# A PSUM bank of its own for the accumulator that is read between block products, in a fused attention and feed-forward kernel

## The chip, the cores and the metric

One core of a Trainium2 chip runs the kernel. The metric is the device time in microseconds of one execution, as the median of several runs. Engines: PE is TensorE (matrix products), DVE is VectorE, ACT is ScalarE, POOL is GpSimd, SP issues the DMAs. PSUM is the memory into which PE writes its products; it has eight banks of 512 fp32 words in each of 128 partitions. SBUF is the working memory.

## The reference

```python
# q, k, v: 4 x 8 x 768 x 64; n_global 8, n_local 96
scores = q @ k.T / sqrt(64)
keep = is_global | is_local                # first 8 positions, or the last 96
scores = where(keep, scores - slope[h] * dist, -1e9)
a = softmax(scores)                        # with 1e-9 added to the sum
x = (a @ v) as 3072 x 512                  # tokens x heads
h = x @ w_in                               # 512 x 2048
g = h * 1 / (1 + exp(-1.702 * h))
out = g @ w_out                            # 2048 x 512, fp32
```

## The kernel before

The 3072 tokens are 24 blocks of 128 rows, two blocks a chunk, so twelve chunks. Every fp32 operand is split into two fp16 halves, high and low, and a product is three fp16 products (high x high, high x low, low x high).

Attention runs block by block: scores on PE (`s`, L522), bias and row minimum on DVE (L528, two passes for two heads), exponentials on ACT (L538), the split into halves on ACT and DVE (`hl`, L542, L543), a transposing DMA (`pt`), and the products with the values on PE (`pv`, L553 to L555). It runs some 60 us ahead of the feed-forward part of the same rows.

The feed-forward part takes each chunk through eight steps of 256 hidden columns. `up` makes `h`, ACT and DVE make the activation and its two halves `g`, and `down` adds its product with `w_out` to the two output accumulators `y` of the chunk (L898). The first three chunks take `up` as it stands. From chunk 3 on (`TWO`), `up_two` takes two steps at once as a 2 x 2 block product by a scheme with seven products in place of eight, the Winograd form: p1 to p7, each of twelve matmuls of 128 x 128. Sums of the blocks of `x` and of the weights are made beforehand (`sums`, `twist`: `xS` and `T`).

In `up_two` an accumulator is read while it is built: p1 is written to `a`, ACT copies it out (k1, L849), p6 is added onto it, ACT copies (k2, L840), p7 is added, DVE adds it to `h1` (q22, L843), p4 is added, and the activation reads it. In the same way p5 is written to `b`, copied (k5, L840), p3 is added, and DVE adds it to `h0` (q12, L843). p2 is only added to `h0` (q11, L843). `a` and `b` are the two halves of one PSUM buffer `ab`, one bank; p2 has a bank for itself. The two banks of a step pair come from the ring `h` or are the accumulators `y10` and `y11`, in turn. Instructions of different engines that touch one PSUM buffer are kept apart by semaphores, in the order in which the program lists them, whichever part of the buffer they touch.

The order is not written by hand. The kernel lists tasks, each with the engines that can do it and a time on each, the tasks it comes after, the buffers it uses and a wished-for time (`add`). `Work.order` goes through a made-up clock: at each moment it gives each free engine the task with the earliest due time among those whose predecessors have ended (plus `LAT`, 0.3, from one engine to another) and whose buffers are to be had. A ring holds so many buffers; a new one is to be had when the last user of the old one has ended. Nothing in that clock knows that two engines cannot be at one bank together. The tasks are then emitted in that order, so every engine's queue has it.

The last chunk's last `down` writes each `y` in two halves of 256 columns, so that the first half can go out earlier: `yo` on DVE or ACT (L912, L913) and a DMA from SP (L914). Both halves lie in one bank. At the end a check of the inputs' size is summed over partitions by one matmul (`pb`, L1052) and read as a flag; the general path behind the flag is not taken here.

Of the kernel before, what the change touches and what calls it, by code (L numbers as in the profile page):

```python
# [19 lines left out]
P = 128  # L20
# [22 lines left out]
class Ring:  # L43


    def __init__(self, pool, tag, bufs, loose=False):
        self.pool, self.tag, self.bufs, self.loose, self.line = pool, tag, bufs, loose, []


class Buf:  # L50


    def __init__(self, ring, shape, dtype, name):
        self.ring, self.shape, self.dtype, self.name = ring, shape, dtype, name
        self.users, self.left, self.end, self.t = [], 0, 0.0, None
        ring.line.append(self)

    def __call__(self):
# [17 lines left out]
class Work:  # L76
# [15 lines left out]
    def order(self):  # L92
# [25 lines left out]
        while len(done) < len(self.tasks) + spared:  # L118
            moved = False
            for e in free:  # L120
                if free[e] > now or (e == "SP" and dma > now + BACKLOG):
                    continue
                best = None
                for t, at in ready.items():
                    if e not in t.on or at > now or t.early() > now or (best is not None and t.due >= best.due):
                        continue
                    us = t.on[e]
                    if any(max(free[o], now) + c < now + us for o, c in t.on.items() if o != e):
                        continue
                    fits = True  # L130
                    for b in t.bufs:
                        if b.left == len(b.users):
                            r = b.ring
                            more = sum(x.left == len(x.users) for x in t.bufs[:t.bufs.index(b)] if x.ring is r)
                            old = r.taken[more - r.bufs] if len(r.taken) + more >= r.bufs > more else None
                            if (r.next != b.i and not r.loose) or (old is not None and (old.left or old.end > now)):
                                fits = False
                                break
                    if fits:
                        best = t  # L140
                if best is None:
                    if e != "PE" or now > WARM or now < worked + (GAP if worked > 7.0 else 0.0):
                        continue
                    best = self.spare(spared)
                    b = best.bufs[0]
                    if len(b.ring.taken) >= b.ring.bufs and (b.ring.taken[-b.ring.bufs].left or b.ring.taken[-b.ring.bufs].end > now):
                        continue
                    b.users, b.left = [best], 1
                    ready[best] = now
                    spared += 1  # L150
                t, us = best, best.on[e]
                del ready[t]
                for b in t.bufs:
                    if b.left == len(b.users):
                        b.ring.next += 1
                        b.ring.taken.append(b)
                t.eng, t.start = e, now
                if e == "SP":
                    free[e] = now + 0.1
                    dma = max(dma, now + 1.2) + us  # L160
                    t.end = dma + 1.0
                else:
                    free[e] = t.end = now + us
                    if e == "PE":
                        worked = t.end
                for b in t.bufs:
                    b.left -= 1
                    b.end = max(b.end, t.end)
                for n in t.next:
                    missing[n] -= 1  # L170
                    if not missing[n]:
                        ready[n] = max(a.end + (LAT if n.on.keys() != {a.eng} else 0.0) for a in n.after)
                done.append(t)
                moved = True
            if not moved:
                later = [x + 1e-6 for x in (t.early() for t in ready) if x > now]
                later += [x for x in (*free.values(), dma - BACKLOG + 1e-6) if x > now] + [at for at in ready.values() if at > now]
                later += [t.end for t in done[-64:] if t.end > now] + ([worked + GAP + 1e-6] if now < worked + GAP else [])
                assert later, "the tasks wait for each other"
                now = min(later)  # L180
        return done
# [13 lines left out]
def kernel(  # L195
# [54 lines left out]


    def ring(tag, bufs, pool=sb, loose=False):
        return Ring(pool, tag, bufs, loose)

    r_raw, r_qk16, r_QK, r_KG = ring("raw", 2), ring("qk16", 1), ring("QK", 3), ring("KG", 1)
    r_VR, r_VG, r_sm = ring("VR", 4), ring("VG", 1), ring("sm", 3)
# [554 lines left out]
    def up_two(c, S, want):  # L811
# [1 line left out]

        nm = f"{c}_{S}"
        rx, rz = (r_h, r_h) if S % 2 == 0 else (r_y[1, 0], r_y[1, 1])
        ab, p2 = Buf(rx, [P, 2, 2, P], F32, "ab" + nm), Buf(rz, [P, 2, P], F32, "p2" + nm)
        h0, h1 = Buf(r_VF, [P, 2, 2, P], F32, "h0" + nm), Buf(r_VF, [P, 2, P], F32, "h1" + nm)
        ts = [Buf(r_t, [P, 2, 2, P], F32, f"t{nm}_{t}") for t in range(2)]
        gg = [Buf(r_g, [P, 2, 2, 2, P], F16, f"g{nm}_{t}") for t in range(2)]
# [2 lines left out]
        half = lambda w, k: (w, lambda z: w()[:, z, 512 * k:512 * k + 512])  # L822
        (B11, B21), B22 = (half(W, 0), half(W, 1)), half(V, 1)
        (T1, T4), (T3, T2) = TT[S, 0], TT[S, 1]
        a, b = (lambda: ab()[:, 0]), (lambda: ab()[:, 1])
        wr = [W_ready[2 * S, 0], W_ready[2 * S + 1, 0], x_ready[2 * c], x_ready[2 * c + 1]]
        tr = [*T_ready[S], xS_ready[c]]

# [8 lines left out]
            return add({"PE": 12 * MM128}, mms, after, [ob, x, wk_[0]], want + due)  # L837

        def keep(o, src, sb_, sp_, after):
            return add({"ACT": 0.3}, lambda e: nc.scalar.copy(o(), src()), after, [sb_, sp_])  # L840

        def plus(o, src, sb_, sp_, after):
            return add({"DVE": 0.34}, lambda e: nc.vector.tensor_add(o(), src(), o()), after, [sb_, sp_])  # L843

        c11, c12 = (lambda: h0()[:, 0]), (lambda: h0()[:, 1])
        p1 = product(a, B11, X, 0, 0, wr, ab, 0.0, first=True)
        p5 = product(b, T1, Xs, 1, 1, [*tr, p1], ab, 0.7)
        p2_ = product(p2, B21, X, 1, 0, wr, p2, 1.4, first=True, last=True)
        k1 = add({"ACT": 0.3}, lambda e: nc.scalar.copy(c11(), a()), [p1, line.get("k1")], [h0, h1, ab])  # L849
        line["k1"] = k1  # L850
        k5 = keep(h1, b, h1, ab, [p5])
        p6 = product(a, T2, Xs, 0, 0, [*tr, k1], ab, 2.1)
        p3 = product(b, B22, Xs, 1, 0, [*tr, *wr, k5], ab, 2.8, last=True)
        q11 = plus(c11, p2, h0, p2, [k1, p2_])
        k2 = keep(c12, a, h0, ab, [p6])
        q12 = plus(c12, b, h0, ab, [k2, p3])
        p7 = product(a, T3, Xs, 0, 1, [*tr, k2], ab, 4.1)
        q22 = plus(h1, a, h1, ab, [p7, k5])
        p4 = product(a, T4, X, 1, 1, [*tr, *wr, q22], ab, 5.5, last=True)
        ups[c, 2 * S] = ups[c, 2 * S + 1] = [p1, p5, p2_, p6, p3, p7, p4]  # L860

        def swish(o, src, srcs, after, w):
# [3 lines left out]
                       [t1], srcs)  # L866

        u0 = [swish(ts[0], h0, [ts[0], h0], [q11, q12], 2)]
        u1 = [swish(lambda: ts[1]()[:, 1], h1, [ts[1], h1], [q22], 1), swish(lambda: ts[1]()[:, 0], a, [ts[1], ab], [p4], 1)]
        for t, u in enumerate((u0, u1)):  # L870
            g, tt = gg[t], ts[t]
            t4 = add({"ACT": 0.53}, lambda e, g=g, tt=tt: nc.scalar.mul(g()[:, 0], tt(), SG / (SX * SW)), u, [tt, g])  # L872
# [3 lines left out]

    def down_two(c, S, want):
        if S == 0:
            ys[c] = [Buf(r_y[0, t], [P, DM], F32, f"y{c}_{t}") for t in range(2)]
        for t in range(2):  # L880
            g, ready = gs[c, S, t]

# [4 lines left out]

    def pile(c, t, g, ready, part, steps, want):

        y, end, begin = ys[c][t], steps[-1] == NST - 1, steps[0] == 0  # L890
        parts = 2 if end and c == NCHUNK - 1 else 1
        w = DM // parts

        def mms(e, m):
            for f in range(2 * len(steps)):
                s = steps[f // 2]
                for j, (zg, z) in enumerate(((0, 0), (0, 1), (1, 0))):
                    nc.tensor.matmul(y()[:, m], part(zg, f), w2(s, z, f % 2)[:, m],  # L898
                                     start=(begin and f + j == 0 and m.start == 0),
                                     stop=(end and j == 2 and f == 2 * len(steps) - 1 and m.stop == DM), skip_group_check=True)  # L900

        f_ = 0.5 / (SG * SW)
        yo = Buf(r_t, [P, DM], F32, f"yo{c}_{t}") if end else None
        last = down_last.get((c, t))
        for p_ in range(parts):
            m = slice(p_ * w, p_ * w + w)
            t1 = add({"PE": 6 * len(steps) * MM512 / parts}, lambda e, m=m: mms(e, m), [*ready, last],
                     [g, y, *(WT[s, 1] for s in steps)], want)
            down_last[c, t] = t1
            if end:  # L910
                t2 = add({"DVE": 0.62, "ACT": 0.5} if parts == 1 else {"DVE": 0.35, "ACT": 0.3}, lambda e, m=m: (
                    nc.vector.tensor_scalar(yo()[:, m], y()[:, m], f_, None, ALU.mult) if e == "DVE" else  # L912
                    nc.scalar.mul(yo()[:, m], y()[:, m], f_)), [t1], [y, yo], want + 4)  # L913
                add({"SP": 0.7 / parts}, lambda e, m=m: nc.sync.dma_start(  # L914
                    out[(2 * c + t) * P:(2 * c + t + 1) * P, m], yo()[:, m]), [t2], [yo], want + 6)

    def down(c, s, want):
        if s == 0:
            ys[c] = [Buf(r_y[c % 2, t], [P, DM], F32, f"y{c}_{t}") for t in range(2)]
        g, ready = gs[c, s]  # L920
        for t in range(2):
            def part(zg, f, t=t):
# [94 lines left out]
    bad = fin[:, 0:1]  # L1017
    ones = const.tile([P, 1], F32, name="ones")
    nc.gpsimd.memset(ones, 1.0)
    pb = Buf(r_s, [P, 512], F32, "pb")  # L1020

    def rows_hold(e):
        nc.vector.tensor_scalar(NM[:, 0:EARLY], top, 1.0 / SC, None, ALU.mult)
# [245 lines left out]
```

## Time and profile before

| | us |
|---|---|
| median of 3 runs | 631.23 (631.23 to 631.97) |
| profiled execution, its own time | 631.02 |
| its span in the profile | 629.2 |
| PE busy | 601.2 (96%) |
| DVE busy | 505.3 (80%) |
| ACT busy | 480.4 (76%) |
| PE at `y`, L898 (1176 matmuls) | 268.2 |

The span runs from the first to the last instruction that the profile shows. Busy time of PE is the union of its matmuls, whose recorded ends are modelled: a matmul of 128 columns is recorded with 0.22 us, though the next starts 0.06 us later. Rows of the timeline give the start, the duration, the engine and line, output and inputs by tile name, the number of merged instructions, and in brackets the idle time ahead and what ended it. The rows of waits give who waited for whom: total, times and the longest, in us.

### The profile page before, as it was taken

How to read it: one execution, taken by the hardware profiler on the slowest of the kernel's cores; microseconds unless marked ns; L12 is line 12 of the kernel's file. 1: busy time of each engine (PE TensorE's matmuls, PEld its weight loads, DVE VectorE, ACT ScalarE, POOL GpSimd, SP SyncE). 2: the span in 40 equal slices, each digit the busy share in tenths (PEclk: the TensorE clock that was granted, in tenths of full speed). 3: DMA queues.
4: the chain of work that ended last, by engine and by line, in shares of the span. 5: the costliest groups of instructions: out<-in, count | busy, mean ns of one | idle time of the engine just before them, and what ended most of it. 6: DMA issues, size and time to landing. Idle time of an engine off the chain costs nothing. (4 is left out here: it accounts for less than half of the span.)

```text
span 629.2 us, 16979 instructions
## 1 busy us (share of the span) xinstructions
PE 601.2 (96%) x6799; PEld 446.9 (71%) x6802; DVE 505.3 (80%) x1176; ACT 480.4 (76%) x1099; POOL 3.9 (1%) x16
## 2 busy tenths in 40 slices
PE   7989998999999999999999999999999999999995
PEld 4877776776776768767668777677777677776663
DVE  5778899999999969778889979869888878766341
ACT  3678999878877978868988879978998977734331
POOL 2000000000000000000000000000000000000000
PEclk9999999999999999999999999999999999999999
DMA  8999797999687778699989999999999997610001
GB/s 192 278 239 321 224 282 148 200 193 167 147 156 131 143 125 158 120 200 194 184 175 221 205 213 192 201 209 188 199 252 204 200 225 168 118 19 2 34 3 37
DMA packets 260854, 108.00 MB, mean 172 GB/s; under 512 B 241665, under 2 KB 242177, under 8 KB 260769
## 3 DMA queue, kind: packets, MB, share of 16 engines
q1 hardware_dynamic: 260480, 106.85, 81.7%
q8 instruction: 54, 0.88, 0.6%
q14 instruction: 32, 0.25, 0.1%
q10 hardware_dynamic: 288, 0.00, 0.0%
HBM read 56.43 MB, written 6.29 MB: 100 GB/s over the span
## 5 line engine op out<-in xcount | busy, mean ns | idle before, releaser
L898 PE MATMUL y<-w,g 128*128 128x512 f16 (+1 forms) x1176 | 268.2, 375 | 0.9 <-DVE g L873 0.9
L898 PEld LDWEIGHTS <-g 128*128 128x128 f16 x1176 | 110.6, 98 | 107.7 <-DVE g L873 1.2
L835 PEld LDWEIGHTS <-w 128*128 128x128 f16 x1728 | 101.6, 98 | 9.3 <-issue 4.8
L835 PEld LDWEIGHTS <-T 128*128 128x128 f16 x1296 | 78.2, 98 | 12.6 <-issue 4.3
L538 ACT ACTIVATE p<-p,NM 128x256 f32<-128x256 f32 (+1 forms) x160 | 77.4, 486 | 5.7 <-DVE NM L528 5.7
L795 PE MATMUL h<-xT,w 128*128 128x256 f16 x576 | 69.7, 273 | 2.3 <-DVE xT L701 1.4
L835 PE MATMUL ab<-xS,T 128*128 128x128 f16 x972 | 67.3, 219 | 3.2 <-ACT h L840 2.2
L543 DVE TENSOR_TENSOR hl<-p,hl 128x512 f16<-128x512 f32 (+1 forms) x80 | 51.9, 648 | 17.2 <-ACT hl L542 16.8
L795 PEld LDWEIGHTS <-w 128*128 128x128 f16 x576 | 55.4, 98 | 12.0 <-issue 2.7
L528 DVE CUSTOM_DVE_ANT_0 p<-s,mm 128x256 f32<-128x256 f32 (+1 forms) x160 | 58.5, 400 | 6.8 <-PE s L522 6.6
L873 DVE SCALAR_TENSOR_TENSOR g<-t,g 128x512 f16<-128x512 f32 x72 | 49.4, 688 | 8.4 <-ACT g L872 7.7
L835 PE MATMUL ab<-xS,w 128*128 128x128 f16 x756 | 51.2, 219 | 3.6 <-ACT h L840 2.9
L872 ACT ACTIVATE g<-t 128x512 f16<-128x512 f32 x72 | 45.3, 630 | 9.5 <-DVE t L865 9.2
L864 ACT ACTIVATE t<-h 128x512 f32<-128x512 f32 (+1 forms) x72 | 36.3, 519 | 18.7 <-DVE h L843 18.6
L542 ACT CAST hl<-p 128x512 f16<-128x512 f32 (+1 forms) x80 | 47.0, 587 | 4.4 <-DMA pt<-hl 2.2
L865 DVE SCALAR_TENSOR_TENSOR t<-t,h 128x512 f32<-128x512 f32 (+1 forms) x72 | 39.1, 555 | 10.0 <-ACT t L864 9.6
L843 DVE TENSOR_TENSOR h<-ab,h 128x256 f32<-128x256 f32 x72 | 29.3, 420 | 14.7 <-PE ab L835 7.9
L522 PEld LDWEIGHTS <-QK 128*128 128x128 f16 x592 | 36.6, 98 | 5.3 <-DVE NM L528 2.7
L840 ACT COPY h<-ab 128x256 f32<-128x256 f32 x72 | 26.2, 371 | 16.2 <-PE ab L835 16.0
L522 PE MATMUL s<-QK 128*128 128x128 f16 x320 | 38.5, 219 | 0.0
L835 PE MATMUL ab<-xT,w 128*128 128x128 f16 x540 | 37.3, 219 | 0.0
L553 PE MATMUL pv<-VR,pt 128*128 128x64 f16 x288 | 33.8, 193 | 2.7 <-DMA pt<-hl 1.8
(190 smaller groups left out, 1074.4 us busy)
## 6 DMA issues: line engine op xcount, KB each, us to landing
ws<-in_moe_w_in_dram SPq DMA_DIRECT2D x8, 1024.0 KB, 6.1
ws<-in_moe_w_out_dram SPq DMA_DIRECT2D x8, 1024.0 KB, 8.1
raw<-in_q_dram SPq DMA_DIRECT2D x24, 256.0 KB, 4.1
raw<-in_k_dram SPq DMA_DIRECT2D x24, 256.0 KB, 4.8
QK<-QK SPq DMA_DIRECT2D x44, 128.0 KB, 4.3
out_dram<-yo SPq DMA_DIRECT2D x22, 256.0 KB, 3.0
raw<-in_v_dram SPq DMA_DIRECT2D x20, 256.0 KB, 3.7
ws_00again<-in_moe_w_in_dram SPq DMA_DIRECT2D x8, 512.0 KB, 5.1
```

The costliest lines, as they stand in the source:

```text
L522: nc.tensor.matmul(sp()[:, j, s * P:(s + 1) * P], d["QK"]()[:, 0, h, :], K[:, 1 + z, h, :], start=(z == 0), stop=(z == 1), skip_group_chec ...
L528: nc.vector.tensor_tensor_reduce(out=pr()[:, j, :], in0=sp()[:, j, :], in1=m, scale=-1.0 / SC, scalar=3.0e38, op0=ALU.add, op1=ALU.min, ac ...
L538: ex.append(add({"ACT": 0.28 + 0.105 * ns}, lambda e, j=j: nc.scalar.activation(pr()[:, j, :], pr()[:, j, :], AF.Exp, bias=NM[:, n, hs[j]: ...
L542: t4 = add({"ACT": 0.1 + 0.215 * ns}, lambda e: nc.scalar.copy(hl()[:, 0], pr()), ex, [pr, hl])
L543: t5 = add({"DVE": 0.07 + 0.265 * ns}, lambda e: nc.vector.tensor_sub(hl()[:, 1], pr(), hl()[:, 0]), [t4], [pr, hl])
L795: nc.tensor.matmul(ph()[:, fi, :], w1(s, cc, z, fi), X[:, y, cc, :], start=(j + cc == 0), stop=(j == 2 and cc == NCC - 1))
L835: nc.tensor.matmul(o()[:, fi], w, x()[:, y * NCC + 2 * k + cc, t], start=(first and fi + j + cc == 0), stop=(last and j + cc == 3), skip_g ...
L864: t1 = add({"ACT": 0.06 + 0.22 * w}, lambda e: nc.scalar.activation(o(), src(), AF.Tanh, scale=0.851 / (SX * SW)), after, srcs)
L865: return add({"DVE": 0.08 + 0.265 * w}, lambda e: nc.vector.scalar_tensor_tensor(o(), o(), 1.0, src(), ALU.add, ALU.mult), [t1], srcs)
L872: t4 = add({"ACT": 0.53}, lambda e, g=g, tt=tt: nc.scalar.mul(g()[:, 0], tt(), SG / (SX * SW)), u, [tt, g])
L873: t5 = add({"DVE": 0.61}, lambda e, g=g, tt=tt: nc.vector.scalar_tensor_tensor(g()[:, 1], tt(), SG / (SX * SW), g()[:, 0], ALU.mult, ALU.s ...
L898: nc.tensor.matmul(y()[:, m], part(zg, f), w2(s, z, f % 2)[:, m], start=(begin and f + j == 0 and m.start == 0), stop=(end and j == 2 and ...
```

## The change

`up_two` gets the buffers `pa` and `pb`, still two banks. `a` is `pa` alone; `pb` holds `b` and, as its second half `g_`, p2. p1 of a step pair also takes hold of `pb` and comes after p1 of the pair before. p6 and p3 are wished for earlier, p2 later, behind p5. The clock of `Work.order` learns of banks: for every PSUM buffer it notes until when PE, and until when the other engines, were at it (plus `LAT`), and a task of PE waits for the others and the reverse. Reads by ACT and DVE are not held apart in it. Some task times are set anew (0.26 for the copies).

In the last chunk each `y` has two buffers of 256 columns from the first step on, the second one in the banks of the rings `s` and `pv`, which are free by then. The check's sum takes its bank from the ring `h`.

```diff
+        self.bank = {}                                   # Buf
...
-                    fits = True
-                    for b in t.bufs:
+
+                    fits = all(b.bank.get(e != "PE", 0.0) <= now for b in t.bufs)
+                    for b in t.bufs if fits else ():
...
+                    if b.ring.psum:
+                        b.bank[e == "PE"] = max(b.bank.get(e == "PE", 0.0), t.end + LAT)
...
-        ab, p2 = Buf(rx, [P, 2, 2, P], F32, "ab" + nm), Buf(rz, [P, 2, P], F32, "p2" + nm)
+        pa, pb = Buf(rx, [P, 2, P], F32, "pa" + nm), Buf(rz, [P, 2, 2, P], F32, "pb" + nm)
...
-        a, b = (lambda: ab()[:, 0]), (lambda: ab()[:, 1])
+        a, b, g_ = pa, (lambda: pb()[:, 0]), (lambda: pb()[:, 1])
...
-            return add({"ACT": 0.3}, lambda e: nc.scalar.copy(o(), src()), after, [sb_, sp_])
+            return add({"ACT": 0.26}, lambda e: nc.scalar.copy(o(), src()), after, [sb_, sp_])
...
-        p1 = product(a, B11, X, 0, 0, wr, ab, 0.0, first=True)
-        p5 = product(b, T1, Xs, 1, 1, [*tr, p1], ab, 0.7)
-        p2_ = product(p2, B21, X, 1, 0, wr, p2, 1.4, first=True, last=True)
-        k1 = add({"ACT": 0.3}, lambda e: nc.scalar.copy(c11(), a()), [p1, line.get("k1")], [h0, h1, ab])
+        p1 = product(a, B11, X, 0, 0, [*wr, line.get("p1")], pa, 0.0, first=True)
+        p1.bufs.append(pb)
+        pb.users.append(p1)
+        line["p1"] = p1
+        p5 = product(b, T1, Xs, 1, 1, tr, pb, 0.7, first=True)
+        k1 = add({"ACT": 0.26}, lambda e: nc.scalar.copy(c11(), a()), [p1, line.get("k1")], [h0, h1, pa])
...
-        p6 = product(a, T2, Xs, 0, 0, [*tr, k1], ab, 2.1)
-        p3 = product(b, B22, Xs, 1, 0, [*tr, *wr, k5], ab, 2.8, last=True)
-        q11 = plus(c11, p2, h0, p2, [k1, p2_])
+        p6 = product(a, T2, Xs, 0, 0, [*tr, k1], pa, 1.4)
+        p3 = product(b, B22, Xs, 1, 0, [*tr, *wr, k5], pb, 2.1, last=True)
+        p2_ = product(g_, B21, X, 1, 0, [*wr, p5], pb, 2.8, last=True)
+        q11 = plus(c11, g_, h0, pb, [k1, p2_])
...
-            ys[c] = [Buf(r_y[0, t], [P, DM], F32, f"y{c}_{t}") for t in range(2)]
+            rings = [[r_y[0, t]] if c < NCHUNK - 1 else [r_y[0, t], (r_s, r_pv)[t]] for t in range(2)]
+            ys[c] = [[Buf(r, [P, DM // len(rs)], F32, f"y{c}_{t}{i}") for i, r in enumerate(rs)] for t, rs in enumerate(rings)]
...
-    pb = Buf(r_s, [P, 512], F32, "pb")
+    pb = Buf(r_h, [P, 512], F32, "pb")
```

Up to the first block product of chunk 3, some 205 us into the span, every engine has the same rows in both orders. PE in the last chunk, second step pair, before (the first matmul of each product alone; the buffer's name has the chunk and the pair): p1, p5, p2, p6, p3, `down`, p7.

```order
L835 MATMUL ab11_1_9680<-xT11_9048,w2_0_532 128x128
...
L835 MATMUL ab11_1_9680<-xS11_9436,T1_2130 128x128
...
L835 MATMUL p211_1_9710<-xT11_9048,w2_0_532 128x128
...
L835 MATMUL ab11_1_9680<-xS11_9436,T1_2130 128x128
...
L835 MATMUL ab11_1_9680<-xS11_9436,w3_0_711 128x128
...
L898 MATMUL y11_0_9754<-w0_1_353,g11_0_0_9644 128x512
```

The same stretch of PE's queue now: p1, p5, p2, p6, one half of the `down`, p3, p7.

```order
L839 MATMUL pa11_1_9680<-xT11_9046,w2_0_532 128x128
...
L839 MATMUL pb11_1_9695<-xS11_9504,T1_2130 128x128
...
L839 MATMUL pb11_1_9695<-xT11_9046,w2_0_532 128x128
...
L839 MATMUL pa11_1_9680<-xS11_9504,T1_2130 128x128
...
L905 MATMUL y11_00_9741<-w0_1_353,g11_0_0_9663 128x256
...
L839 MATMUL pb11_1_9695<-xS11_9504,w3_0_711 128x128
```

p3 followed p6 directly; now twelve half-wide matmuls of `down` stand between, and p6 and p3 are in different buffers.

DVE's end of queue before: the last activations and halves `g` of the last chunk, with one output piece `yo` in front of the last `g`.

```order
L843 TENSOR_TENSOR h111_3_10013<-ab11_3_9957,h111_3_10013 128x256
L865 SCALAR_TENSOR_TENSOR t11_3_1_10074<-t11_3_1_10074,h111_3_10013 128x256
L865 SCALAR_TENSOR_TENSOR t11_3_1_10074<-t11_3_1_10074,ab11_3_9957 128x256
L912 TENSOR_SCALAR yo11_0_10117<-y11_0_9754 128x256
L873 SCALAR_TENSOR_TENSOR g11_3_1_10115<-t11_3_1_10074,g11_3_1_10115 128x512
```

DVE's end of queue now:

```order
L847 TENSOR_TENSOR h111_3_10065<-pa11_3_10003,h111_3_10065 128x256
L872 SCALAR_TENSOR_TENSOR t11_3_0_10117<-t11_3_0_10117,h011_3_10038 128x512
L872 SCALAR_TENSOR_TENSOR t11_3_1_10120<-t11_3_1_10120,h111_3_10065 128x256
L880 SCALAR_TENSOR_TENSOR g11_3_0_10148<-t11_3_0_10117,g11_3_0_10148 128x512
L872 SCALAR_TENSOR_TENSOR t11_3_1_10120<-t11_3_1_10120,pa11_3_10003 128x256
L880 SCALAR_TENSOR_TENSOR g11_3_1_10165<-t11_3_1_10120,g11_3_1_10165 128x512
```

The output piece has left DVE's queue; all four stand on ACT, behind its last work on `g`.

More of the change, by code (lines that the diff above doesn't have):

```diff
@@ L43, with __init__ @@
 class Ring:
-    def __init__(self, pool, tag, bufs, loose=False):
-        self.pool, self.tag, self.bufs, self.loose, self.line = pool, tag, bufs, loose, []
+    def __init__(self, pool, tag, bufs, loose=False, psum=False):
+        self.pool, self.tag, self.bufs, self.loose, self.line, self.psum = pool, tag, bufs, loose, [], psum
 class Buf:
@@ L177, in order @@
                 later += [x for x in (*free.values(), dma - BACKLOG + 1e-6) if x > now] + [at for at in ready.values() if at > now]
-                later += [t.end for t in done[-64:] if t.end > now] + ([worked + GAP + 1e-6] if now < worked + GAP else [])
+                later += [x for t in done[-64:] for x in (t.end, t.end + LAT) if x > now] + ([worked + GAP + 1e-6] if now < worked + GAP else [])
                 assert later, "the tasks wait for each other"
@@ L252, in ring @@
     def ring(tag, bufs, pool=sb, loose=False):
-        return Ring(pool, tag, bufs, loose)
+        return Ring(pool, tag, bufs, loose, pool is ps)
     r_raw, r_qk16, r_QK, r_KG = ring("raw", 2), ring("qk16", 1), ring("QK", 3), ring("KG", 1)
@@ L845, in up_two @@
         c11, c12 = (lambda: h0()[:, 0]), (lambda: h0()[:, 1])
-        p1 = product(a, B11, X, 0, 0, wr, ab, 0.0, first=True)
-        p5 = product(b, T1, Xs, 1, 1, [*tr, p1], ab, 0.7)
-        p2_ = product(p2, B21, X, 1, 0, wr, p2, 1.4, first=True, last=True)
-        k1 = add({"ACT": 0.3}, lambda e: nc.scalar.copy(c11(), a()), [p1, line.get("k1")], [h0, h1, ab])
-        line["k1"] = k1
-        k5 = keep(h1, b, h1, ab, [p5])
-        p6 = product(a, T2, Xs, 0, 0, [*tr, k1], ab, 2.1)
-        p3 = product(b, B22, Xs, 1, 0, [*tr, *wr, k5], ab, 2.8, last=True)
-        q11 = plus(c11, p2, h0, p2, [k1, p2_])
[L855 to L859, printed above, removed]
+        p1 = product(a, B11, X, 0, 0, [*wr, line.get("p1")], pa, 0.0, first=True)
[4 more added lines that the diff above has]
+        k1 = add({"ACT": 0.26}, lambda e: nc.scalar.copy(c11(), a()), [p1, line.get("k1")], [h0, h1, pa])
+        line["k1"] = k1
+        k5 = keep(h1, b, h1, pb, [p5])
+        p6 = product(a, T2, Xs, 0, 0, [*tr, k1], pa, 1.4)
+        p3 = product(b, B22, Xs, 1, 0, [*tr, *wr, k5], pb, 2.1, last=True)
+        p2_ = product(g_, B21, X, 1, 0, [*wr, p5], pb, 2.8, last=True)
+        q11 = plus(c11, g_, h0, pb, [k1, p2_])
+        k2 = keep(c12, a, h0, pa, [p6])
+        q12 = plus(c12, b, h0, pb, [k2, p3])
+        p7 = product(a, T3, Xs, 0, 1, [*tr, k2], pa, 4.1)
+        q22 = plus(h1, a, h1, pa, [p7, k5])
+        p4 = product(a, T4, X, 1, 1, [*tr, *wr, q22], pa, 5.5, last=True)
         ups[c, 2 * S] = ups[c, 2 * S + 1] = [p1, p5, p2_, p6, p3, p7, p4]
@@ L868, in up_two @@
         u0 = [swish(ts[0], h0, [ts[0], h0], [q11, q12], 2)]
-        u1 = [swish(lambda: ts[1]()[:, 1], h1, [ts[1], h1], [q22], 1), swish(lambda: ts[1]()[:, 0], a, [ts[1], ab], [p4], 1)]
+        u1 = [swish(lambda: ts[1]()[:, 1], h1, [ts[1], h1], [q22], 1), swish(lambda: ts[1]()[:, 0], a, [ts[1], pa], [p4], 1)]
         for t, u in enumerate((u0, u1)):
@@ L888, in pile, with mms @@
     def pile(c, t, g, ready, part, steps, want):
[L890 to L894, printed above, removed]
+        end, begin = steps[-1] == NST - 1, steps[0] == 0
+        w = DM // len(ys[c][t])
+        def mms(e, y, m):
             for f in range(2 * len(steps)):
@@ L897, in mms @@
                 for j, (zg, z) in enumerate(((0, 0), (0, 1), (1, 0))):
-                    nc.tensor.matmul(y()[:, m], part(zg, f), w2(s, z, f % 2)[:, m],
-                                     start=(begin and f + j == 0 and m.start == 0),
-                                     stop=(end and j == 2 and f == 2 * len(steps) - 1 and m.stop == DM), skip_group_check=True)
+                    nc.tensor.matmul(y(), part(zg, f), w2(s, z, f % 2)[:, m], start=(begin and f + j == 0),
+                                     stop=(end and j == 2 and f == 2 * len(steps) - 1), skip_group_check=True)
         f_ = 0.5 / (SG * SW)
         yo = Buf(r_t, [P, DM], F32, f"yo{c}_{t}") if end else None
[L904 to L909, printed above, removed]
+        for i, y in enumerate(ys[c][t]):
+            m = slice(i * w, i * w + w)
+            t1 = add({"PE": 6 * len(steps) * MM512 * w / DM}, lambda e, y=y, m=m: mms(e, y, m), [*ready, down_last.get((c, t, i))],
+                     [g, y, *(WT[s, 1] for s in steps)], want + 0.1 * i)
+            down_last[c, t, i] = t1
             if end:
[L911 to L914, printed above, removed]
+                t2 = add({"DVE": 0.08 + 0.54 * w / DM, "ACT": 0.06 + 0.44 * w / DM}, lambda e, y=y, m=m: (
+                    nc.vector.tensor_scalar(yo()[:, m], y(), f_, None, ALU.mult) if e == "DVE" else
+                    nc.scalar.mul(yo()[:, m], y(), f_)), [t1], [y, yo], want + 4)
+                add({"SP": 0.7 * w / DM}, lambda e, m=m: nc.sync.dma_start(
                     out[(2 * c + t) * P:(2 * c + t + 1) * P, m], yo()[:, m]), [t2], [yo], want + 6)
@@ L918, in down @@
         if s == 0:
-            ys[c] = [Buf(r_y[c % 2, t], [P, DM], F32, f"y{c}_{t}") for t in range(2)]
+            ys[c] = [[Buf(r_y[c % 2, t], [P, DM], F32, f"y{c}_{t}")] for t in range(2)]
         g, ready = gs[c, s]
```

## The prediction

> **What bounds the kernel now.** I read the page first, then stretches, then TensorE's own waits, then the timeline at the places those waits name. The page: span, busy time, and the tenths over 40 slices.
>
> ```profile
> span 629.2 us, 16979 instructions
> PE 601.2 (96%) x6799; PEld 446.9 (71%) x6802; DVE 505.3 (80%) x1176; ACT 480.4 (76%) x1099; POOL 3.9 (1%) x16
> ...
> PE   7989998999999999999999999999999999999995
> DVE  5778899999999969778889979869888878766341
> ACT  3678999878877978868988879978998977734331
> PEclk9999999999999999999999999999999999999999
> ```
> TensorE (PE) is busy 601.2 of 629.2 us at full granted clock, VectorE (DVE) and ScalarE (ACT) hold sevens to nines. So a change pays only by what it takes out of PE's idle time or of the two ends. The next rows cut the span where the block products begin and where the last output pieces are left; the second number is PE's busy time.
>
> ```profile
> 0.00:205.00 205.00, 193.93 (x1767) 145.56 (x1771) 180.71 (x365) 162.61 (x288) 3.90 (x16) 1.00 0.90 206
> 205.00:618.50 413.50, 403.88 (x5008) 298.77 (x5006) 323.54 (x810) 316.77 (x809) 0.00 (x0) 1.00 0.80 158
> 618.50:629.20 10.70, 3.42 (x30) 2.58 (x28) 1.02 (x2) 1.04 (x3) 0.00 (x0) 0.87 0.17 54
> ```
> Up to 205 us the order of every engine is the same in both programs but for names, so those 11 idle us stay. In the middle 413.5 - 403.9 = 9.6 us are idle; behind 618.5 lies the tail. What PE waits for from 205 on (us in total, times, longest):
>
> ```profile
> PE ab L835 <- ACT h L840: 5.2, 11, 0.9
> PE pv L553 <- DMA pt<-hl: 1.8, 4, 0.9
> PE ab L835 <- DVE h L843: 1.5, 2, 0.8
> PE y L898 <- DVE g L873: 0.9, 1, 0.9
> PE pv L553 <- DMA VR<-VG: 0.8, 1, 0.8
> ```
> Two thirds (5.2 + 1.5 = 6.7 us, 13 times) is a block product that waits until ACT or DVE has read the bank `ab`. One such wait, in the second step pair of the last chunk (PE rows are p1, p5, p2, p6, p3, then `down`):
>
> ```profile
> 584.69 0.83 PE L835 MATMUL ab<-xT,w 128*128 128x128 f16 x12
> 585.36 0.83 PE L835 MATMUL ab<-xS,T 128*128 128x128 f16 x12
> 586.03 0.83 PE L835 MATMUL p<-xT,w 128*128 128x128 f16 x12
> 586.23 0.37 ACT L849 COPY h<-ab 128x256 f32<-128x256 f32 x1 [0.96 <-PE ab L835]
> 586.70 0.83 PE L835 MATMUL ab<-xS,T 128*128 128x128 f16 x12
> 586.98 0.42 DVE L843 TENSOR_TENSOR h<-p,h 128x256 f32<-128x256 f32 x1 [1.24 <-PE p L835]
> 587.57 0.37 ACT L840 COPY h<-ab 128x256 f32<-128x256 f32 x1 [0.44 <-PE ab L835]
> 588.00 0.83 PE L835 MATMUL ab<-xS,w 128*128 128x128 f16 x12 [0.46 <-ACT h L840]
> 588.66 2.75 PE L898 MATMUL y<-w,g 128*128 128x512 f16 x12
> ```
> The copy k1 (L849) needs p1's half alone, whose matmuls ended at 584.69 + 0.83 = 585.52, yet starts at 586.23, 0.04 behind p5's end: the halves share a bank, and accesses to a bank are kept apart. p6, in the first half, is followed directly by p3, in the same bank; k5 (L840, 587.57) runs only when p6 has drained, and p3 starts at 588.00, 0.06 behind k5's end. In the stream p3 was due at 586.70 + 0.67 = 587.37 (p2 to p6 is 0.67 start to start, though one is recorded with 0.83), so the loss is 0.63 to 0.67: the idle 0.46 plus 0.16 to 0.2 of pipeline that drains. Each wait above thus costs its idle time plus 0.16.
>
> The other kind: a copy late because its engine was busy.
>
> ```profile
> 404.30 0.19 PE L553 MATMUL pv<-VR,pt 128*128 128x64 f16 x1
> ...
> 404.62 0.19 PE L555 MATMUL pv<-VR,pt 128*128 128x64 f16 x1
> 404.69 0.63 ACT L392 ACTIVATE junk<-raw 128x512 bf16<-128x512 f32 x1
> 405.20 0.20 ACT L392 ACTIVATION_READ_ACCUMULATOR junk<-raw 128x1 f32 x1
> 405.30 0.37 ACT L840 COPY h<-ab 128x256 f32<-128x256 f32 x1
> 405.72 0.83 PE L835 MATMUL ab<-xS,T 128*128 128x128 f16 x12 [0.90 <-ACT h L840]
> ```
> The product at 405.72 had twelve value products (404.30 to 404.65) ahead of it; its copy (405.30) stood behind a check of raw input (0.63 and its 0.20 read).
>
> **The change, part by part.** *Bank of its own (`pa`), p2 beside b (`pb`), new order.* The round trip that a product must cover is drain 0.16, hop 0.04, copy 0.37, hop 0.06: 0.63 to 0.67, one product. I counted in both orders, at each bank read by ACT or DVE, how much PE work stands between the product read and the product that waits for the read, priced by rows: 0.67 a product, 2.75 - 0.16 = 2.6 for twelve matmuls of `down`, 0.35 for twelve of values (404.30 to 404.62 + 0.03), 0.67 x 8 / 12 = 0.45 for eight of scores. Before: 5 places with nothing between, 4 with 0.35 to 0.45, 15 with 0.67 to 0.79, 8 with 1.02. After: none under 0.90, 8 from 0.90 to 1.02, the rest from 1.1 up. Every place that loses time by distance alone is gone; the 13 rows and their drains are 6.7 + 13 x 0.16 = 8.8 us. What remains is the second kind, a copy behind a long ACT instruction. Eight places have 0.23 to 0.4 us of slack, less than an instruction of 0.63; if a third of them lose 0.4 that is 1.0 us, and I take that. Ends: 0 left (8.8 saved), and only the five bare places saved (5 x 0.67 = 3.4). I stand near the first: 13 waits in all against 32 places under 1.1 us means that most places with hardly any slack show none. Sum: -7.8.
>
> *Reads of `pb`.* p2's bank was its own, so q11 (DVE, 0.42, row 586.98) and k5 met nowhere. Now both read `pb` and take turns ahead of p3: 0.16 + 0.04 + 0.42 + 0.06 + 0.37 + 0.06 = 1.1 us from p2's end. Where both stand ahead of p3 in the new order, the smallest PE work between is 1.35 us, mostly 1.7 to 4.8. I cost it at 0, covered by `down` and attention matmuls; without that cover it is 0.4 per place. The bounds are -0.2 and +3.
>
> The Trainium skill's page "PSUM — Partial Sum Buffer", section "PSUM bank collisions raise a hardware error", speaks against this part: two engines must not touch one bank at once, reads against reads included, so putting p2 beside b makes two readers exclude each other that were free. By that rule alone, 36 steps with 0.48 each would add 17 us if nothing covered them. The trace agrees in kind (k1's 586.23 waits for a write to the other half), but no run here shows two readers held apart.
>
> *A wait that becomes visible: values.* PE also waits for `pt` and `VR` from DMA, 1.8 + 0.8 us in five waits, 3.4 with drains. The DMA engines are at their fullest here (last numbers: granted clock, DMA share, GB/s):
>
> ```profile
> 450.00:500.00 50.00, 48.97 (x605) 35.89 (x603) 42.78 (x107) 46.20 (x120) 0.00 (x0) 1.00 1.09 212
> ```
> The work between a unit's scores and its value products is 8.1 us or more in the old order and 7.7 or more in the new; under 9 us are 6 of 78 units then, 10 now. Scaled, 3.4 becomes 5.7; and PE reaches them sooner, since it loses less in between. Ends: -1.0 (other places, none tight) and +4 (each of the ten tight ones 0.7). I take +1.5, nearer to the scaled +2.3 than to nothing. Queued behind a late `pt` on PE are the block products, so ACT's copies come late too, with no further loss.
>
> *One new neighbour.* In block 12 to 13 a group of scores follows another with one product between, and waits for two row passes of DVE:
>
> ```profile
> L528 DVE CUSTOM_DVE_ANT_0 p<-s,mm 128x256 f32<-128x256 f32 (+1 forms) x160 | 58.5, 400 | 6.8 <-PE s L522 6.6
> ```
> Block 12 opens a batch and its rows are half as long, so about 0.2 + 0.04 + 2 x 0.3 + 0.06 = 0.9 against 0.67: +0.2 (0 to 0.5).
>
> *The last output in four banks.* The tail before:
>
> ```profile
> 616.97 0.42 DVE L865 SCALAR_TENSOR_TENSOR t<-t,ab 128x256 f32<-128x256 f32 x1 [2.03 <-ACT t L864]
> 617.42 0.63 ACT L872 ACTIVATE g<-t 128x512 f16<-128x512 f32 x1 [0.49 <-DVE t L865]
> 619.17 0.42 DVE L912 TENSOR_SCALAR yo<-y 128x256 f32<-128x256 f32 x1 [1.78 <-PE y L898]
> 619.51 0.68 DVE L873 SCALAR_TENSOR_TENSOR g<-t,g 128x512 f16<-128x512 f32 x1
> 619.62 4.52 SPq L914 DMA_DIRECT2D out_dram<-yo  x4
> 620.25 2.57 PE L898 MATMUL y<-w,g 128*128 128x256 f16 x22 [0.90 <-DVE g L873]
> 622.92 0.66 ACT L913 ACTIVATE yo<-y 128x256 f32<-128x256 f32 x2 [2.85 <-PEq L1069]
> ```
> `yo` (619.17) waited 1.78 us on DVE until both halves of its bank were written, and behind it in DVE's queue the last `g` (619.51), for which PE waited 0.90 (620.25); with the drain 1.06. In the new order all four pieces are evacuated by ACT, no `yo` stands ahead of that `g` on DVE, and two rounds of `down` (5.3 us) stand between the last product and the piece that needs it, against a chain of 0.4 + 0.4 + 0.6 + 0.7 plus hops, 2.5 us. So -1.06 (0 to -1.06). At the very end two pieces (622.92, 0.66) are copied when PE is done, since they share a bank; now one: 0.66 - 0.38 = -0.28 (0 to -0.6, if the output DMA queue, two issues late, gains too). The pieces of 256 columns: 22 take 2.57, (2.57 - 0.27) / 21 = 0.1095 each; twelve of 512 take (2.75 - 0.38) / 11 = 0.2155. Two halves cost 0.0035 more; three of four step pairs of the last chunk change, 72 matmuls of 512 columns: +0.25 (0 to 0.3).
>
> *No time:* the check's bank taken from another ring (its matmul has 3 columns and nobody on PE waits for its reader); other cost numbers only shape the order already counted; the banks in use stay eight.
>
> Sum: -7.8 + 1.5 + 0.2 - 1.06 - 0.28 + 0.25 = -7.2 us. The profiled execution took 631.02 us, 0.2 below the median 631.23, which a median may add again: 631.02 - 7.2 = 623.8.
>
> **Rivals.** (a) *Nothing takes its place:* all 8.8 of the bank waits and part of the 3.4 of values go: 631.0 - 8.8 - 1.06 - 0.28 + 0.25 = 621.1, and 617.7 if values lose nothing either. For it: no place without slack is left. Against: ACT is busy 8 to 9 tenths there, and rows like 405.30 will not all vanish.
>
> (b) *Handed on to DMA:* PE arrives sooner at `pt`, transposes do not come sooner, at a DMA share of 1.09. Twenty units that wait 0.3 more, 6 us, take back most: 629. For it the row of 450 to 500; against it that an average of 11.2 us of PE work stands between scores and values in both orders, and that scores too move forward with PE.
>
> (c) *The order changes nothing that counts:* the waits of before come from busy engines and reappear elsewhere: 630 to 632. Against it, the five bare places and their rows.
>
> (d) *Slower, by the shared bank of two readers:* k5 behind q11 holds p3, p3 holds `h0`'s last sum and the whole activation chain. It decides where p2-to-p3 work averages under about 0.9 us, so that 36 steps lose over 0.25 each beyond the 9 saved; with 0.5 each on top of the losses of before: 631 + 18 - 8.8 - 1.3 = 639. Against it: 1.35 is the least in the order.
>
> **How the numbers follow.** My forecast (621.5 to 627) has 0.60, (a) below 621.5 has 0.17, (b) 627 to 630 has 0.10, (c) 0.06, (d) 0.07. This kernel's runs tell 0.2% (1.3 us) from no change; so faster is 0.60 + 0.17 + 0.10 = 0.87, same 0.06, slower 0.07. The range 618.5 to 629.0 leaves out the extreme of (a), about 0.04, the upper edge of (b), 0.03, and (c) and (d).
>
> **What would show it.** Right: TensorE's waits for `pa` and `pb` from ACT and DVE together under 2 us from 205 on; none longer than 0.7 by distance; no wait for the last `g`; one copy behind PE's last matmul; PE idle of the middle stretch 9.6 down to 3 to 5. Values' waits 3 to 5 us with drains. Wrong: waits of `pv` for `pt` over 6 us (b); `pb` products that wait for a copy that itself waited for DVE (d); PE idle time unchanged (c).

## The result and the profile after

The changed kernel takes 621.32 us (619.98 to 621.72, six runs) against 631.49 (629.93 to 631.97) of the kernel before beside it: 0.9837 of the time, 95% interval 0.9822 to 0.9852. The forecast was 623.8, range 618.5 to 629.0. The profiled execution took 621.17 us with a span of 619.4, so the span is 9.8 shorter. The page of the changed kernel, the same rows as before:

```profile
span 619.4 us, 17131 instructions
PE 599.5 (97%) x6871; PEld 453.0 (73%) x6874; DVE 503.8 (81%) x1175; ACT 480.1 (78%) x1100; POOL 3.9 (1%) x16
...
PE   7989998999999999999999999999999999999995
```

No engine's work has become less to speak of; the digits of PE had no hole before and have none now. Most of what changed shows in PE's idle time, span less busy time: 28.0 us before, 19.9 now. The stretches (span, then PE's busy time):

```profile
0.00:205.00 205.00, 193.51 (x1754) 144.51 (x1758) 180.12 (x365) 162.45 (x285) 3.89 (x16) 1.00 0.93 206
205.00:608.00 403.00, 400.99 (x5077) 304.28 (x5074) 323.72 (x811) 316.12 (x812) 0.00 (x0) 1.00 0.83 162
608.00:619.40 11.40, 5.02 (x46) 4.24 (x44) 0.00 (x0) 1.54 (x4) 0.00 (x0) 0.83 0.17 52
```

The head lost 11.5 us as before (11.1). The middle's idle time went from 9.6 us to 403.00 - 400.99 = 2.0. PE's waits from 205 us on, of which five rows stood before:

```profile
PE pv L557 <- DMA pt<-hl: 1.5, 2, 1.0
PE s L526 <- DVE NM L532: 0.2, 1, 0.2
```

No row for `pa` or `pb` is left, none for the last `g`; values and one group of scores remain. The signs named beforehand came, two of them stronger than foretold: the idle time of the middle is 2.0 (foretold 3 to 5), and the values lose 2.9 us with drains (3 to 5). The same step pair that the prediction showed (chunk 11, second pair):

```profile
577.60 0.83 PE L839 MATMUL pa<-xT,w 128*128 128x128 f16 x12
...
578.27 0.83 PE L839 MATMUL pb<-xS,T 128*128 128x128 f16 x12
578.47 0.37 ACT L855 COPY h<-pa 128x256 f32<-128x256 f32 x1 [0.29 <-PE pa L839]
...
578.94 0.83 PE L839 MATMUL pb<-xT,w 128*128 128x128 f16 x12
579.61 0.83 PE L839 MATMUL pa<-xS,T 128*128 128x128 f16 x12
579.88 0.42 DVE L847 TENSOR_TENSOR h<-pb,h 128x256 f32<-128x256 f32 x1 [1.25 <-PE pb L839]
...
580.28 1.47 PE L905 MATMUL y<-w,g 128*128 128x256 f16 x12
580.34 0.37 ACT L844 COPY h<-pb 128x256 f32<-128x256 f32 x1 [0.97 <-DVE h L847]
...
581.59 0.83 PE L839 MATMUL pb<-xS,w 128*128 128x128 f16 x12
```

The copy k1 (578.47) starts 0.04 behind p1's own end (577.60 + 0.83) while p5 is running into the other bank; before it waited for p5 as well. In `pb` the sum q11 (579.88) and the copy k5 (580.34) take turns, 0.04 apart. p3 (581.59) could have come behind k5's end at 580.71, and PE does not notice, since half a `down` of 1.31 us stands between p6 and p3. So the program does make the two readers take turns, and the order covers it with work that had to be done anyway.

The end, in which all four pieces are copied by ACT:

```profile
605.00 8.02 PE L905 MATMUL y<-w,g 128*128 128x256 f16 x72
...
606.84 0.69 DVE L880 SCALAR_TENSOR_TENSOR g<-t,g 128x512 f16<-128x512 f32 x1 [0.69 <-ACT g L879]
609.18 0.38 ACT L918 ACTIVATE yo<-y 128x256 f32<-128x256 f32 x1 [2.37 <-PE y L905]
609.60 4.20 SPq L919 DMA_DIRECT2D out_dram<-yo  x4
...
613.05 0.39 ACT L918 ACTIVATE yo<-y 128x256 f32<-128x256 f32 x1 [0.87 <-PE y L905]
```

The last `g` (606.84 to 607.53) is ready long before the matmuls that need it, and PE runs through its last 72 matmuls unbroken. One piece is copied behind PE's end (613.02) where there were two. Yet from PE's end to the span's end it is 619.4 - 613.0 = 6.4 us, as before (622.82 to 629.2). The copies end 0.3 earlier after PE, but what stands between the last copy and the end is 0.4 longer (5.6 before, 6.0 now). The four output DMAs took longer to land; their row before, then after (number, KB each, median us from issue to landing):

```profile
out_dram<-yo SPq DMA_DIRECT2D x4, 128.0 KB, 2.1
```

```profile
out_dram<-yo SPq DMA_DIRECT2D x4, 128.0 KB, 3.2
```

### The profile page after: what moved, and what is told of

Its sections match the earlier page's. It is cut to its first block, busy times and chain, and to the rows that moved or that the text cites. A ratio compares the mean times of both kernels' runs of the same rounds, so it can differ in the third digit from the quotient of the medians.

```text
span 619.4 us, 17131 instructions
## 1 busy us (share of the span) xinstructions
PE 599.5 (97%) x6871; PEld 453.0 (73%) x6874; DVE 503.8 (81%) x1175; ACT 480.1 (78%) x1100; POOL 3.9 (1%) x16
## 4 chain that ended last, share of the span: by engine, by line
PE 72%; DVE 11%; DMA 8%; ACT 5%; issue 3%; SPq 0%; POOL 0%; DVEq 0%; ACTq 0%; POOLq 0%
PE y L905 31%; PE pa L839 12%; PE pb L839 9%; PE h L799 8%; PE s L526 4%; DMA pt<-hl 4%; DMA QK<-qk 1%; PE pv L557 1%; DVE w L367 1%; PE pv L559 1%; PE pv L558 1%; PE pv L633 1%; ACT p L542 1%; DMA raw<-in_k_dram 1%; DVE hl L547 1%
## 5 line engine op out<-in xcount | busy, mean ns | idle before, releaser
L905 PEld LDWEIGHTS <-g 128*128 128x128 f16 x1248 | 117.6, 98 | 102.1 <-DVE g L811 1.1
L839 PEld LDWEIGHTS <-T 128*128 128x128 f16 x1296 | 76.6, 98 | 4.5 <-issue 0.2
L847 DVE TENSOR_TENSOR h<-pb,h 128x256 f32<-128x256 f32 x72 | 29.1, 419 | 28.5 <-PE pb L839 26.5
L839 PE MATMUL pa<-xS,T 128*128 128x128 f16 x648 | 45.0, 219 | 0.0
L839 PE MATMUL pb<-xS,w 128*128 128x128 f16 x540 | 37.5, 219 | 0.0
L839 PE MATMUL pa<-xT,w 128*128 128x128 f16 x540 | 37.2, 219 | 0.0
L526 PE MATMUL s<-QK,QK 128*128 128x128 f16 x272 | 33.9, 219 | 2.0 <-DVE NM L532 2.0
```

The lines of the kernel that those rows point to most:

```text
L526: nc.tensor.matmul(sp()[:, j, s * P:(s + 1) * P], d["QK"]()[:, 0, h, :], K[:, 1 + z, h, :], start=(z == 0), stop=(z == 1), skip_group_chec ...
L839: nc.tensor.matmul(o()[:, fi], w, x()[:, y * NCC + 2 * k + cc, t], start=(first and fi + j + cc == 0), stop=(last and j + cc == 3), skip_g ...
L905: nc.tensor.matmul(y(), part(zg, f), w2(s, z, f % 2)[:, m], start=(begin and f + j == 0), stop=(end and j == 2 and f == 2 * len(steps) - 1 ...
```

## The experiments

The change has three parts: the order that knows of banks, the bank of its own (`pa`, and p2 beside b), and the four banks of the last output. The first four runs take them apart; the kernel before took 631.42 us beside them.

**The bank without the order.** The changed kernel, its made-up clock blind to banks:

```diff
-        return Ring(pool, tag, bufs, loose, pool is ps)
+        return Ring(pool, tag, bufs, loose, False)
```

> The changed kernel, with the two buffers pa and pb, but the order is made without knowledge of banks. If the order is what counts (theory O): in this order nine places have a copy of pb behind DVE's read of pb with too little PE work between, 8 x 0.47 + 0.2 + 0.1 = 4.1 us, so TensorE waits 4 to 6 us for pa and pb and the time is 625 to 627. If the bank of its own is what counts (theory B): waits under 1.5 us, 621 to 622.5.

Measured: 625.75 us (624.01 to 626.39), 0.9906 [0.9889, 0.9923], in the range of theory O, with waits a little under its 4 to 6 us. PE's waits from 205 us on, and the same step pair of the last chunk:

```profile
PE pb L839 <- DVE h L847: 3.5, 10, 0.7
PE pv L557 <- DMA VR<-VG: 2.1, 1, 2.1
PE pv L557 <- DMA pt<-hl: 1.0, 3, 0.5
```

```profile
582.46 0.83 PE L839 MATMUL pb<-xT,w 128*128 128x128 f16 x12
583.12 0.83 PE L839 MATMUL pa<-xS,T 128*128 128x128 f16 x12
583.33 0.37 ACT L844 COPY h<-pb 128x256 f32<-128x256 f32 x1 [0.44 <-PE pb L839]
583.73 0.42 DVE L847 TENSOR_TENSOR h<-pb,h 128x256 f32<-128x256 f32 x1 [1.58 <-ACT h L844]
...
584.21 0.83 PE L839 MATMUL pb<-xS,w 128*128 128x128 f16 x12 [0.25 <-DVE h L847]
```

This is the mechanism of rival (d): k5 (583.33) and q11 (583.73) read different halves, q11 needs nothing of k5's, yet it starts 0.03 behind k5's end, and p3 (584.21) behind both. p3 was due at 583.12 + 0.67 = 583.79, so one place costs 0.42. Seven of the ten waits listed are of this kind, 2.0 us together. In the other three (1.5 us, the longest among them) k5 had ended before q11 began; q11 stood behind other work of DVE, and p3 waited for it because it reads the same bank. No wait for `pa` is listed. A bank of its own thus takes away the old waits and makes new ones, unless the order puts other work between.

**The order without the bank.** The kernel before, with nothing but the bookkeeping of banks in its clock; `ab`, `p2` and the last output stay:

```diff
+                    fits = all(b.bank.get(e != "PE", 0.0) <= now for b in t.bufs)
+                    for b in t.bufs if fits else ():
...
+                    if b.ring.psum:
+                        b.bank[e == "PE"] = max(b.bank.get(e == "PE", 0.0), t.end + LAT)
```

> The kernel before, with ab and p2 as they were and the last output as it was; only the order's simulation keeps banks whole. Theory O: this order has 5 places with less than 1.1 us between in place of 32, so TensorE's waits for ab fall from 6.7 us to 1 to 2, the last g still comes late (1.06): 622.5 to 624.5. Theory B: a and b still exclude each other, and waits are traded for a longer order: 628 to 631.

Measured: 622.56 us (621.75 to 625.27), 0.9867 [0.9846, 0.9889]. The order alone brings 8.9 of the 10 us, as theory O had it, though the last `g` came in time, where the expectation had it late:

```profile
PE pv L556 <- DMA pt<-hl: 3.2, 3, 1.3
PE s L525 <- DVE NM L531: 1.0, 2, 0.6
PE ab L838 <- ACT h L843: 0.8, 1, 0.8
PE ab L838 <- DVE h L846: 0.5, 1, 0.5
PE pv L556 <- DMA VR<-VG: 0.2, 1, 0.2
```

With one shared bank, 6.7 us in 13 waits became 1.3 in two. So most of these waits come from an order that puts a reader and a writer of a bank next to each other without knowing it, and go though a and b still share the bank. A later run of the shared bank, below, keeps more of them.

**The last output as before.** The changed kernel with the halves of each last `y` in one bank again (one buffer for each `t` in `down_two`; the matmuls and copies of `pile` go back with it):

```diff
-            rings = [[r_y[0, t]] if c < NCHUNK - 1 else [r_y[0, t], (r_s, r_pv)[t]] for t in range(2)]
+            ys[c] = [Buf(r_y[0, t], [P, DM], F32, f"y{c}_{t}") for t in range(2)]
...
```

> The changed kernel with the last output as before (halves of one bank, in the last step pair alone). If the four banks gained by the last g (theory T): PE waits again 0.9 us for it and two pieces are copied at the end, 621.3 + 1.06 + 0.28 = 622.6. Rival: the tail behind TensorE's end is the same and the order finds other work: 621.0 to 621.6.

Measured: 621.78 us (621.13 to 622.03), 0.9851 [0.9835, 0.9867], not told apart from the whole change. The time lies between the two theories, but the wait for the last `g` that theory T expected back is not among PE's waits.

**Four banks alone.** The kernel before with only the last output in four banks (the same lines the other way round, and the check's bank):

> The kernel before with nothing changed but the last output in four banks. Theory T: 631.5 - 1.06 - 0.28 + 0.25 = 630.4; TensorE's waits for ab stay at 6 to 7 us. Rival (the four banks are nothing): 631.2 to 631.8.

Measured: 628.98 us (627.58 to 629.70), 0.9957 [0.9943, 0.9972]: 2.4 us less than before, and 1.4 less than theory T.

```profile
PE ab L835 <- ACT h L840: 4.2, 9, 0.9
...
PE ab L835 <- DVE h L843: 1.2, 2, 0.8
```

The wait for the last `g` is gone, and two bank waits fewer are listed (11 in place of 13). The two that are gone, 0.46 and 0.52 us at 597.94 and 609.16 in the kernel before, stood in the last chunk, where the order came out otherwise. Theory T had not counted them. Under the order that knows of banks this part has nothing left to take, since that order alone already moved `yo` behind the last `g` on DVE.

**Bank or order, once more, and the values.** Two questions were open. Is the separate bank worth anything once the order knows of banks? And what sets the waits of the value products, the term that went the other way than foretold? Next the changed kernel ran again, then the whole change but with `ab` shared and p2 alone (the order's experiment plus four banks), then the changed kernel with a DMA believed to land later in the made-up clock, which makes the order leave more work between a unit's scores and its values:

```diff
-                    t.end = dma + 1.0
+                    t.end = dma + (1.0 if now < 150.0 else 1.8)
```

The changed kernel again:

> The changed kernel once more, beside the next two on the same chip: 621.3, within 0.7 of it.

`ab` shared, order with banks, four banks at the end:

> The kernel before with the order that keeps banks whole and with the last output in four banks, but a and b still share one bank and p2 has its own: the whole change but its title. In this order 3 places have 1.02 us between, none less. Theory O (PE work between read and next product is all that counts): 621.0 to 622.3, waits for ab under 1 us. Theory B2 (the bank of its own is worth something beyond what the order does): 623 or more, waits for ab of 2 us or more.

Later landings:

> The changed kernel whose order takes a DMA to land 0.8 us later from 150 us on, so that the least PE work between a unit's scores and its value products is 9.6 us in place of 7.7. If values wait because too little PE work stands ahead of them (theory D): the losses at values from 205 us on fall from 2.9 us to under 1.0, and the time by 1.5 to 2.5 to 619 to 620. Rival: other transfers are late just then (queue behind large loads), whatever the order: losses of 2 to 3.5 us, 620.8 to 622.

Measured beside 630.84 us of the kernel before: the changed kernel 621.70 (618.74 to 622.05), 0.9846 [0.9824, 0.9868]; shared 623.18 (622.25 to 623.91), 0.9877 [0.9860, 0.9894]; later landings 619.48 (617.57 to 620.73), 0.9823 [0.9801, 0.9844]. The waits of the last two:

```profile
PE pv L556 <- DMA pt<-hl: 4.3, 5, 1.5
PE ab L838 <- ACT h L843: 0.8, 1, 0.8
PE s L525 <- DVE NM L531: 0.7, 1, 0.7
```

```profile
PE pa L839 <- DVE h L847: 0.8, 1, 0.8
PE pb L839 <- DVE h L847: 0.6, 1, 0.6
```

With the shared bank, one wait for `ab` came back, 0.8 us; most of the rest of the difference is at values and scores, whose places follow from the order that came out. By its time the run lies in the range of theory B2, by its waits in that of theory O, so it settles neither. With later landings no wait for `pt` is listed, as theory D had it, and two for block products appear that the changed kernel did not have.

**The three that followed.** Later landings again; the shared bank with later landings (1.7, from the same clock time on), whose order has no place without slack; and later landings with a clock that keeps every two engines apart at a bank, readers among them:

```diff
-                    fits = all(b.bank.get(e != "PE", 0.0) <= now for b in t.bufs)
+                    fits = all(x <= now for b in t.bufs for o, x in b.bank.items() if o != e)
...
-                        b.bank[e == "PE"] = max(b.bank.get(e == "PE", 0.0), t.end + LAT)
+                        b.bank[e] = max(b.bank.get(e, 0.0), t.end + LAT)
```

Later landings, a second time:

> The changed kernel with the later landings once more, for the next two to be set beside: 619.5, within 1.

Shared bank with later landings:

> The shared bank (a and b in ab, p2 apart) with the order that keeps banks whole, the four banks at the end, and DMAs taken to land 0.7 us later from 150 us on. This order has no place without slack and at least 9.1 us between scores and values. Theory O (the bank of its own adds nothing once the order is good; the last shared-bank run lost its time at values): losses at values under 1.2 us, waits for ab under 1.5, 619.0 to 620.7, as the kernel with pa and pb. Theory B2 (the bank itself is worth 1.5 us): 621.3 or more.

Every two engines kept apart:

> The changed kernel with later landings (0.8 us) and an order that also keeps ACT and DVE apart at a bank. If the two waits of 0.6 to 0.8 us on DVE that the later landings brought are readers that met at pb (theory R): they go, 618.5 to 619.3. If they are DVE's queue (rival Q: one is for pa, where nobody else reads): they stay or move, 619.3 to 620.7.

Measured beside 630.72 us of the kernel before: 618.80 (617.54 to 621.43), 0.9814 [0.9791, 0.9837]; shared 624.30 (622.95 to 625.67), 0.9895 [0.9878, 0.9913]; every two apart 619.23 (619.05 to 619.51), 0.9818 [0.9802, 0.9833]. The second profile of the later landings has other waits than the first, from the same program:

```profile
PE pv L557 <- DVE h L847: 0.9, 1, 0.9
PE pa L839 <- ACT h L844: 0.6, 1, 0.6
PE pv L557 <- DMA pt<-hl: 0.4, 1, 0.4
```

The shared bank fell short. The view that distances in the order decide, and the bank does not matter, expected it level with its sister, and it is 5 us slower. Its waits, and the longest of them:

```profile
PE ab L838 <- ACT h L843: 2.6, 3, 1.1
PE ab L838 <- DVE h L846: 1.8, 3, 0.9
...
PE ab L838 <- ACT h L852: 0.3, 1, 0.3
```

```profile
310.27 0.19 PE L558 MATMUL pv<-VR,pt 128*128 128x64 f16 x1
310.37 0.62 ACT L875 ACTIVATE g<-t 128x512 f16<-128x512 f32 x1
...
310.89 0.36 ACT L852 COPY h<-ab 128x256 f32<-128x256 f32 x1
311.14 0.38 ACT L843 COPY h<-ab 128x256 f32<-128x256 f32 x1
...
311.57 0.83 PE L838 MATMUL ab<-xS,T 128*128 128x128 f16 x12 [1.11 <-ACT h L843]
```

Both copies are late, because ACT's queue had a `g` (310.37) ahead of them. The product at 311.57 follows the two copies, so it is p6, which needs the first one alone (L852, ended 311.25). It waited for the second (L843, ended 311.52) because that reads the other half of the same bank. This is the second kind of wait in the prediction, a busy engine, and there the bank counts: with one bank a late copy holds the next product whichever half it reads. But by these rows the bank's part is 311.52 - 311.25 = 0.27 of the 1.11 us; the rest is ACT's queue, which another bank would not shorten. The part can be larger: at 407.85 a product, p7 by its place in the queue, waits for a sum of DVE (407.38 + 0.42) that reads the other half, while the copy it needs had ended at 407.00. The seven waits at `ab` are 4.7 us in all, and how much of the 5 us between the two runs is the bank's stays open.

Keeping every two engines apart in the clock brought nothing in sum: 619.23 beside 619.48 and 618.80. Its waits:

```profile
PE s L526 <- DVE NM L532: 2.0, 2, 1.2
PE pb L839 <- DVE xS L735: 1.2, 3, 0.4
PE pv L557 <- DMA pt<-hl: 0.9, 1, 0.9
PE pa L839 <- DVE h L847: 0.2, 1, 0.2
```

The waits for a sum `h` fell from 1.4 to 0.2, and scores and a late `xS` took their place. Two things keep this from deciding between theory R and rival Q. The two waits in question are not in the second profile of the later landings either, so they do not belong to that order alone. And this order differs from the start: PE idles 8.0 us up to 205 us and 4.3 from there to 608, where the first profile of the later landings has 10.8 and 1.5.

## Why the prediction was right, and where it was not

Right in sign and mechanism: PE lost its time where a read of a bank had no more than one product's length of work to hide behind. The size came out larger, 9.8 us between the spans where 7.2 was foretold. To compare the terms I count a loss as the time from one matmul's start to the next beyond the usual pitch of that kind, so that the pipeline's drain is in it, for gaps over 0.06 us from 205 us on:

| loss of PE, us | before | after | change | foretold |
|---|---|---|---|---|
| block products at a bank | 9.5 | 0.5 | -9.0 | -7.8 |
| values (`pv`) | 3.9 | 2.9 | -0.9 | +1.5 |
| scores (`s`) | 0 | 0.6 | +0.6 | +0.2 |
| last `g` | 1.1 | 0 | -1.1 | -1.06 |

With the estimate of 0.25 for the half-width matmuls this makes -10.1, against a span shorter by 9.8. One of the thirteen waits, 0.46 us behind the two matmuls of the inputs' check, is not in the 9.5, since those have no usual pitch; against it, the head up to 205 us idled 0.4 longer in the profile after.

**Bank waits, -7.8:** I left 1.0 us for copies behind long ACT instructions; 0.5 was left, and 0.2 of that is a wait for a sum `xS`, not for a bank. I had counted the places with 0.23 to 0.4 us of slack in the order's text, and took a third of them to lose; hardly any did.

**Reads of `pb`, 0:** right, but for a reason that the order supplies. The run that kept the bank and took away the order's knowledge showed 3.5 us of waits behind a reader of `pb`, in ten places, so rival (d) is a true mechanism whose condition did not hold. The Trainium skill's page "PSUM — Partial Sum Buffer", section "PSUM bank collisions raise a hardware error", has the rule that two engines' reads of one bank must be kept apart. The traces show that this program keeps them apart, by its semaphores: 579.88 + 0.42 to 580.34 in the changed kernel, 583.33 + 0.37 to 583.73 in the blind one. No run here shows what two reads at once would do. The 17 us that I worked out for turns with nothing to cover them were an upper bound; 3.5 us is what came in the blind order.

**Values, +1.5: the step that failed.** I scaled the waits by the number of units with little PE work ahead of their values, and added that PE reaches them sooner. Over all profiles the second half is not borne out. Where the made-up clock lets a DMA land after 1.0, the values lost 2.4 to 5.1 us in eight profiles, with no clear tie to how much PE lost elsewhere: 3.9 and 4.1 in the two kernels that lose 9 us at banks, 2.4 to 3.3 in the two profiles of the changed kernel and the one with the old output, 4.2 to 5.1 with the blind order or a shared bank. So the 6 us of rival (b), the gain handed on to the DMAs, were seen in no run; an effect of 1 us could hide in the differences between the orders. With landings 1.7 or 1.8 the values lost 0.7, 1.9, 0.8 and 1.2 in four profiles: more distance in the order takes most of this term away, and the least distances of 8.1 us before and 7.7 after were too close together to tell which way it would go.

**The end:** the last `g` as foretold. The last copy's -0.28 did not show in this pair: PE's end to the span's end is 6.4 us in both. Over all profiles it does: that stretch is 6.3 to 6.7 us, 6.5 in the mean, in the three profiles with two pieces at the end, and 5.8 to 6.5, 6.2 in the mean, in the nine with one. What made it long in the profile after is open. The median landing of the output DMAs does not tell: with 1.8 in the run with the last output as before, 5.8 us lie between the last copy and the end, and with 2.1 in the kernel before, 5.6.

**The sum:** the time is 2.5 us under 623.8. Bank waits make 1.2 of it and values 2.4, with 0.4 of scores, 0.3 at the end and the 0.4 of the head against them. So 621.32 lies in the range, but on the ground of rival (a), in which nothing takes the waits' place (621.1, below 621.5), and the reason given for it, that no place without slack is left, held.

**What each part is worth.** The order alone is worth 8.9 us, the four banks alone 2.4, the bank of its own with four banks and the blind order 5.7; together they are worth 10.2, since each cures some of the same waits. Given the order, the four banks add nothing that can be told. What the bank of its own adds given the order depends on the order that comes out: 0.8 (622.56 to 621.78, not told apart), 1.5 (623.18 to 621.70) and 5 (624.30 to 619.48 and 618.80, with landings 1.7 and 1.8). Every pair also differs in its order, so the bank's share by itself stays open.

The version with later landings has the lowest medians: 0.9823 and 0.9814 of the time before, where the change has 0.9837 and 0.9846. Its medians lie 2 to 3 us under those of the change, by these ratios it is 1 to 2 us; the intervals overlap, so it is not shown that it beats the change.

## What to carry to other kernels

Where engines are kept apart by whole banks, an order made by a simulated clock must know it: a reader and a writer of one bank next to each other in a queue cost a full round trip (here 0.63 to 0.67 us a place), and here telling the clock was worth more than another bank (8.9 us, against 5.7 for the bank with the four banks at the end and a blind order). A bank of its own spares a product the wait for a late reader of the other half (0.27 us of the 1.11 at 311.57); what it is worth over a whole kernel is not settled here, and what shares the other bank must be looked at as readers that take turns. Waits for a DMA depend on how much work the order leaves ahead of them: here a later landing in the clock took the loss at values from 2.4 to 5.1 us down to 0.7 to 1.9.

## Of the hardware, not expected

The landing of the four small output DMAs at the end (128 KB each) had a median of 1.8 to 3.2 us in the nine profiles with four banks. The times of one program spread as well: the changed kernel, run again, took from 618.74 to 622.05 us. Of the 1.9 us between the spans of its two profiled executions (619.4 and 617.5) PE's losses from 205 us on account for 0.5, the stretch behind PE's end for 0.4 (6.4 and 6.0), and the head for 0.9: the first block product starts at 204.84 and at 203.97, in the same order. So the head alone moves a comparison by about as much as the smaller effects here, and a difference of 2 us between two orders needs more than one profile of each.
